# Four interleaved attention layers on one core: the builder orders VectorE's and GpSimd's latest instructions together in time

## The chip, the cores and the metric

One core of a Trainium2 chip. The metric is the device time of one execution in microseconds (us). Engines: TensorE (PE in the profile) multiplies and writes its results to banks of PSUM; its weight loads are PEld. ScalarE (ACT) evaluates exponentials, VectorE (DVE) and GpSimd (POOL) do elementwise work, SyncE (SP) issues transfers.

## The reference

An input x of 2048 tokens by 512 goes through four layers in turn, each x + f(layernorm(x)), with 32 heads of 16:

```python
x = x + _A_ref(_layernorm(x), A_wq, A_wk, A_wv, A_wo, A_beta)
x = x + _B_ref(_layernorm(x), B_wqkv, B_wo)
x = x + _A_ref(_layernorm(x), A_wq, A_wk, A_wv, A_wo, A_beta)
x = x + _B_ref(_layernorm(x), B_wqkv, B_wo)
```

B is plain attention over all 2048 tokens: softmax(q k^T / 4) v, then the output projection. A cuts the tokens into four segments of 512. Inside a segment it is causal attention; beside it stands a memory, read with phi(q) M / (phi(q) z) and then updated with phi(k)^T v, where phi(t) is t + 1 above zero and exp(t) below. A gate per head, sigmoid(beta), mixes the two. The segments of A are a chain through M and z; a segment of a layer needs only what the layer before it has finished.

## The kernel before, in words

Nothing of the program is written in its final order by hand. A Python class, `Builder`, walks through the work and calls `Sched.add` for each instruction; `Sched` keeps a list for each engine, finds what each instruction must wait for, and estimates on a model clock (`estimate`, line 128) when it would end. The builder's choices read this clock: `late("dve")`, for instance, is how far VectorE's model time is past TensorE's. The emitted program is the five lists; the clock itself leaves nothing in it.

**Units.** Scores are made in tiles of 128 keys by 512 queries for one head, one bank of PSUM each. A *unit* (`unit`, line 1752) is two or three tiles: their score products (`ps<-qm,KB` in layers 2 and 4, `ps<-qm,KA` in layers 1 and 3), then one exponential on ScalarE over all of them (line 1829, 1024 or 1536 wide) to the tile pT, then, two units later, the products with V. Two sets of three banks alternate, so a unit's scores wait for the exponential two units before.

**Tiles on VectorE.** When a unit has only two tiles for ScalarE, VectorE may take a tile or two into other banks (`dx_first`, line 1306). It reads the scores from PSUM, scales them and writes 16-bit integers whose bits are an approximation of the exponential (line 1314, 512 or 1024 wide). Two more versions of it are made by adding constants (`EXP_STEPS`), and TensorE multiplies all three with V and sums them: three products for such a tile, one for a tile of ScalarE. The buffers are dxt and, where they are free, borrowed ones named KA, QA, VA, wA and wB.

**The two additions** run on either engine. `task_dx` and `dx_four` (lines 1352, 1389) put them on VectorE (line 1370, 1024 integers for a pair of tiles; line 1403, 2048 for two pairs) unless `pool_copy` (line 1377) puts them on GpSimd (line 1385, 512 words of 32 bits, one instruction for each pair). It does so when GpSimd's model time is less than a limit, POOL_D or POOL_C, past VectorE's.

**Background work** comes between units: normalization, projections, the memory, output projections, loads. Tasks are generators that give up control with a price (`bg_one`, line 1482). Whether one may run next is decided by limits and by the model clock.

**Limits.** `PLAN` has one row for each 20 units (units 0 to 1528, rows 0 to 76). `set_limits` loads a row when its first unit begins: how late VectorE may be, how many tiles of a group it may take, when banks count as free, and some 60 more.

**The port.** VectorE and GpSimd can hold each other up. Before the change, `estimate` keeps the last eight intervals of GpSimd and the last sixteen of VectorE's instructions without PSUM (`held`, `taken`). An instruction that is added is moved behind an interval of the other engine that was added before it. It then stays where it is, even if an instruction that is added later to the other engine begins earlier in model time.

Of the kernel before, what the change touches and what calls it, by code (L numbers as in the profile page):

```python
# [7 lines left out]
ALU = mybir.AluOpType  # L8
# [3 lines left out]
D = 512  # L12
# [21 lines left out]
PORT = 140  # L34

LAG = {"pe": 100, "act": 60, "dve": 60, "pool": 70, "sp": 50}
# [51 lines left out]
class Sched:  # L88
# [4 lines left out]
    def __init__(self):  # L93
        self.ops = {e: [] for e in ENGS}
        self.t = {e: 0.0 for e in ENGS}
        self.tiles = []

        self.streams, self.cover = [], 0.0
        self.recent, self.over, self.pe_end, self.floor = [], [0.0, 0.0], 0.0, 0.0
        self.held, self.taken, self.port, self.raw = [], [], False, False  # L100
        self.pe_seen, self.pe_no, self.pe_at = {}, [0], [0.0]
# [261 lines left out]
class Builder:  # L363
# [15 lines left out]
        12: dict(R_LATE=1500, DX_LATE=500, REST=12, NEAR=8, R_NEAR=50, PV_SKIP=500, FILL_DVE=400, BUSY_ROOM=900, CR_W=1300, DX_LAG=1, LOW=20, HOLD_SEGS=2, BACK=6, R_PAIRS=2, TRADE=0, HOLD_MAX=0),
        13: dict(R_LATE=1500, DX_LATE=500, REST=12, NEAR=8, R_NEAR=50, PV_SKIP=500, FILL_DVE=400, BUSY_ROOM=900, CR_W=1300, DX_LAG=1, LOW=20, HOLD_SEGS=2, BACK=6, R_PAIRS=2, TRADE=0, HOLD_MAX=0),  # L380
        14: dict(MARGIN=500, NEAR=12, PV_SKIP=100, FILL_DVE=200, BUSY_ROOM=300, FILL=0.55, CR_W=1500, CARRY_W=400, R_PAIRS=2, OPART=3, GAP=3, DVE_LATE=800, QMIN=1, POOL_QM=1, SLACK=350, R_NEAR=10, CR_B=1800, QWAIT=8, LN1_AT=6, CR_A=1200, POOL_D=2500, POOL_WAIT=0),
        15: dict(MARGIN=500, NEAR=12, PV_SKIP=100, FILL_DVE=200, BUSY_ROOM=300, FILL=0.55, CR_W=1500, CARRY_W=400, R_PAIRS=2, OPART=3, GAP=3, DVE_LATE=800, QMIN=1, POOL_QM=1, PAIRS=999, SLACK=350, R_NEAR=10, CR_B=1800, QWAIT=8, LN1_AT=6, CR_A=1200, POOL_D=2500, POOL_WAIT=0, POOL_C=2000, PACE=12),
        16: dict(DX_BANK=900, SLACK=350, PV_SKIP=100, EARLY=100, FILL_DVE=200, BUSY_ROOM=300, BACK=6, FILL=0.55, CR_W=1500, PART=3, R_PAIRS=2, TAKEN=0.3, DVE_LATE=800, LN1_AT=6, BUSY_BACK=800, MARGIN=500, LOW=30, POOL_C=2000, OPART=3, GAP=3, PAIRS=24, R_NEAR=10, QWAIT=8, CR_A=1200, POOL_D=2500, PHI_LATE=0, QMIN=1, NEAR=12, POOL_QM=1),
        17: dict(MARGIN=400, NEAR=3, PV_SKIP=100, FILL_DVE=100, BUSY_ROOM=900, FILL=0.55, CR_W=1500, CARRY_W=400, R_PAIRS=2, OPART=4, GAP=3, DVE_LATE=800, QMIN=1, HOLD_AT=40, POOL_QM=1, ACT1=300, DX_LATE=900, REST=8, CR_B=1800, DX_LAG=1, BACK=6, QWAIT=3, POOL_C=2000, LOW=14, BUSY_WAIT=500, SLACK=350, PART=3, BUSY_BACK=800, R_NEAR=10, POOL_D=2500, PHI_LATE=0),
        18: dict(MARGIN=400, NEAR=3, PV_SKIP=100, FILL_DVE=100, BUSY_ROOM=900, FILL=0.4, CR_W=1500, CARRY_W=400, R_PAIRS=2, OPART=4, GAP=3, DVE_LATE=800, QMIN=1, HOLD_AT=40, POOL_QM=1, ACT1=300, DX_LATE=900, REST=8, CR_B=1800, DX_LAG=1, BACK=6, QWAIT=3, POOL_C=0, LOW=14, BUSY_WAIT=500, POOL_D=1200, PART=3, PHI_LATE=0, REST_A=20, EVAC_ACT=800),
        19: dict(MARGIN=400, NEAR=3, PV_SKIP=100, FILL_DVE=100, BUSY_ROOM=900, FILL=0.4, CR_W=1500, CARRY_W=400, R_PAIRS=2, OPART=4, GAP=3, DVE_LATE=800, QMIN=1, HOLD_AT=40, POOL_QM=1, ACT1=300, DX_LATE=900, REST=8, CR_B=1800, DX_LAG=1, BACK=6, QWAIT=3, POOL_C=0, LOW=14, BUSY_WAIT=500, POOL_D=1200, PART=3, PHI_LATE=0, REST_A=20, EVAC_ACT=800),
        20: dict(MARGIN=400, NEAR=3, PV_SKIP=100, FILL_DVE=100, BUSY_ROOM=900, FILL=0.4, CR_W=1500, CARRY_W=400, R_PAIRS=2, OPART=4, GAP=3, DVE_LATE=800, QMIN=1, HOLD_AT=40, POOL_QM=1, ACT1=300, DX_LATE=900, REST=8, CR_B=1800, DX_LAG=1, BACK=6, QWAIT=3, POOL_C=1, LOW=14, BUSY_WAIT=500, POOL_D=1200, PART=3, PHI_LATE=0, EVAC_ACT=800),
        21: dict(MARGIN=400, NEAR=3, PV_SKIP=100, FILL_DVE=100, BUSY_ROOM=900, FILL=0.4, CR_W=1500, CARRY_W=400, R_PAIRS=2, OPART=3, GAP=3, DVE_LATE=800, QMIN=1, HOLD_AT=40, POOL_QM=1, ACT1=300, DX_LATE=900, REST=8, CR_B=1800, DX_LAG=1, BACK=2, QWAIT=3, POOL_C=0, LOW=14, BUSY_WAIT=500, POOL_D=1200, R_NEAR=10),
        22: dict(DX_LATE=900, R_NEAR=10, EARLY=0, BUSY_ROOM=900, FILL=0.57, OPART=4, MASK_PE=200, DIV_LATE=2500, DVE_LATE=800, BG_BANK=400, QMIN=4, HOLD_SEGS=2, PHI_LATE=0, POOL_QM=1, DX_BANK=700, SLACK=700, BACK=6, PART=3, LN1_AT=3, BUSY_BACK=800, POOL_XN=1, NEAR=5, LOW=30, ACT1=300, REST=20, PV_SKIP=900, CR_B=1800, R_PAIRS=2, DX_LAG=1, QWAIT=3, CARRY_W=400, MARGIN=400, POOL_C=1),
# [62 lines left out]
    NEARW = 60  # L452
# [1793 lines left out]
```

## Time and profile before

| | |
|---|---|
| median of 3 runs | 1702.32 us (1701.98 to 1706.57) |
| profiled execution | 1705.54 us, span 1703.8 us |
| granted TensorE clock, mean | 0.997 |
| ScalarE busy | 1656.1 us, 97% of the span |
| TensorE busy | 1603.3 us, 94% |
| VectorE busy | 1472.4 us, 86% |
| GpSimd busy | 966.7 us, 57% |

A row of a group reads: line, engine, operation, output<-inputs, shapes, count | busy us, mean ns of one | idle time of the engine just before them, and what ended it. Neighbouring instructions of one engine overlap, so a mean can be longer than the distance from one start to the next. TensorE's busy time includes products with zeros that the builder puts into its gaps.

### The profile page before, as it was taken

The page shows a single profiled execution, that of the slowest core. Times are in us where ns is not written, and L with a number is a line of the kernel's source. Part 1 is how long each engine was busy: PE and PEld are TensorE (multiplying, and loading weights), DVE is VectorE, ACT ScalarE, POOL GpSimd, SP SyncE. Part 2 cuts the span into 40 slices and gives each one's busy share as a digit, 9 for nine tenths or more (in the row PEclk, how much of TensorE's full clock was granted, in tenths as well). Part 3 has the DMA queues.
Part 4 walks back from the last instruction along what each step waited for, and adds up shares of the span by engine and source line. Part 5 has one row for each costly group of instructions (what it writes and reads, how often), then busy time and mean ns, then how long its engine had stood idle before and what let it go on. Part 6 is the DMA issues. An engine that isn't in the chain of part 4 may idle for free.

```text
span 1703.8 us, 45449 instructions
## 1 busy us (share of the span) xinstructions
PE 1603.3 (94%) x19699; PEld 570.6 (33%) x19699; DVE 1472.4 (86%) x2555; ACT 1656.1 (97%) x1574; POOL 966.7 (57%) x1057
## 2 busy tenths in 40 slices
PE   8998989999999999999899999999999999999999
PEld 5553435322222232434235222432222222222226
DVE  6667776999999999887977899889999999999996
ACT  8899999999999999999899999999999999999998
POOL 2333212358966555411652865566688866668995
PEclk9999999999999999999999999999999999999999
DMA  6210201001112001222132112001001100100000
GB/s 180 39 21 20 46 13 36 5 14 23 23 21 52 17 14 33 55 68 51 48 60 30 31 38 53 14 14 51 2 17 20 45 17 17 14 10 17 17 14 18
DMA packets 148424, 54.46 MB, mean 32 GB/s; under 512 B 128768, under 2 KB 147712, under 8 KB 148224
## 3 DMA queue, kind: packets, MB, share of 16 engines
q1 hardware_dynamic: 148224, 51.56, 14.0%
q8 instruction: 154, 2.52, 0.6%
q14 instruction: 46, 0.38, 0.1%
HBM read 18.88 MB, written 2.10 MB: 12 GB/s over the span
## 4 chain that ended last, share of the span: by engine, by line
ACT 53%; PE 26%; DVE 16%; POOL 3%; issue 1%; DMA 0%; ACTq 0%; SPq 0%; POOLq 0%; DVEq 0%
ACT pT L1829 52%; PE ps L626 25%; DVE KA L1314 3%; DVE dxt L1314 3%; DVE wA L1314 1%; DVE wB L1314 1%; ACT amem L903 1%; DVE dxt L1370 1%; POOL dxt L1385 1%; DVE lnst L801 1%; POOL QA L1385 1%; DVE x L1152 0%; DVE xn L830 0%; DVE wB L1403 0%; POOL pT L1843 0%
## 5 line engine op out<-in xcount | busy, mean ns | idle before, releaser
L1829 ACT ACTIVATE pT<-ps 128x1024 bf16<-128x1024 f32 (+1 forms) x1529 | 1625.2, 1221 | 35.8 <-PE ps L626 31.4
L626 PE MATMUL ps<-qm,KB 32*128 32x512 bf16 x4096 | 566.3, 385 | 66.8 <-ACT pT L1829 42.0
L626 PE MATMUL ps<-pT,VB 128*17 128x512 bf16 x2810 | 485.7, 385 | 3.9 <-DVE ub L688 0.7
L1385 POOL TENSOR_TENSOR dxt<-dxt,shift 128x512 int32<-128x512 int32 (+1 forms) x237 | 252.3, 1074 | 244.1 <-DVE dxt L1370 128.7
L626 PEld LDWEIGHTS ps<-qm,KB 32*128 32x128 bf16 x4096 | 144.8, 91 | 584.3 <-ACT pT L1829 445.0
L1314 DVE TENSOR_SCALAR KA<-ps 128x512 uint16<-128x512 f32 (+1 forms) x424 | 310.9, 753 | 16.8 <-PE ps L626 15.1
L1314 DVE TENSOR_SCALAR dxt<-ps 128x512 uint16<-128x512 f32 (+1 forms) x341 | 249.8, 749 | 18.4 <-PE ps L626 17.0
L626 PE MATMUL ps<-dxt,VB 128*17 128x512 bf16 x1089 | 235.7, 382 | 0.2 <-POOL dxt L1385 0.2
L1385 POOL TENSOR_TENSOR VA<-KA,shift 128x512 int32<-128x512 int32 (+1 forms) x177 | 187.5, 1067 | 80.2 <-DVE QA L1370 43.1
L626 PEld LDWEIGHTS ps<-pT,VB 128*17 128x17 bf16 x2810 | 113.1, 87 | 280.2 <-issue 261.2
L1843 POOL TENSOR_SCALAR_AFFINE_SELECT pT<-pT 128x512 bf16<-128x512 bf16 (+4 forms) x134 | 73.9, 563 | 222.7 <-ACT pT L1829 222.7
L1385 POOL TENSOR_TENSOR QA<-KA,shift 128x512 int32<-128x512 int32 (+1 forms) x109 | 119.9, 1107 | 65.6 <-DVE KA L1314 62.4
L1385 POOL TENSOR_TENSOR wB<-wB,shift 128x512 int32<-128x512 int32 (+1 forms) x105 | 110.1, 1059 | 43.9 <-DVE wB L1370 17.8
L626 PE MATMUL ps<-QA,VB 128*17 128x512 bf16 x460 | 132.8, 383 | 0.0
L626 PE MATMUL ps<-VA,VB 128*17 128x512 bf16 x460 | 131.3, 382 | 0.5 <-POOL VA L1385 0.4
L1385 POOL TENSOR_TENSOR wA<-wA,shift 128x512 int32<-128x512 int32 (+1 forms) x94 | 101.8, 1092 | 42.9 <-DVE wA L1370 22.9
L1314 DVE TENSOR_SCALAR wB<-ps 128x512 uint16<-128x512 f32 (+1 forms) x157 | 115.4, 752 | 7.5 <-PE ps L626 7.1
L626 PE MATMUL ps<-KA,VB 128*17 128x512 bf16 x460 | 118.9, 383 | 0.0
L1314 DVE TENSOR_SCALAR wA<-ps 128x512 uint16<-128x512 f32 (+1 forms) x142 | 109.2, 786 | 7.2 <-PE ps L626 6.5
L626 PE MATMUL ps<-wA,VB 128*17 128x512 bf16 x486 | 113.0, 384 | 0.3 <-POOL wA L1385 0.2
L626 PE MATMUL ps<-wB,VB 128*17 128x512 bf16 x519 | 112.5, 390 | 0.1
L626 PE MATMUL ps<-qm,KA 32*128 32x128 bf16 (+2 forms) x1536 | 95.3, 254 | 13.7 <-ACT pT L1829 10.1
(172 smaller groups left out, 2166.6 us busy)
## 6 DMA issues: line engine op xcount, KB each, us to landing
wB<-in_B_wqkv_dram SPq DMA_DIRECT2D x48, 128.0 KB, 2.4
wA<-in_A_wk_dram SPq DMA_DIRECT2D x16, 128.0 KB, 2.3
wA<-in_A_wq_dram SPq DMA_DIRECT2D x16, 128.0 KB, 2.2
wA<-in_A_wv_dram SPq DMA_DIRECT2D x16, 128.0 KB, 2.4
out_dram<-x SPq DMA_DIRECT2D x8, 256.0 KB, 2.2
x<-in_A_x_dram SPq DMA_DIRECT2D x3, 512.0 KB, 9.4
wB<-in_B_wqkv_dram SPq DMA_DIRECT2D x1, 1536.0 KB, 12.8
oT<-ob SPq DMA_TRANSPOSE x63, 2.5
```

The lines of the kernel that those rows point to most:

```text
L626: self.sc.add("pe", lambda e: e.matmul(out, lhsT, rhs, start=start, stop=stop, skip_group_check=True), reads=reads, banks=[(bank, "w", all ...
L801: self.op("dve", (lambda i, t: lambda e: e.bn_stats(st[:, k, i, 0:6], self.x[:, t, :]))(i, t), reads=[self.b_x[t]], writes=[bs], ns=690, p ...
L903: self.op("act", lambda e: e.activation(et, src, ACT.Exp), reads=bsrc, writes=self.b_amem, ns=1023, gap=915)
L1314: self.op("dve", lambda e: e.tensor_scalar(d, o, SCALE * LOG2E * 128, 127.0 * 128 + EXP_BIAS, op0=ALU.mult, op1=ALU.add), writes=self.b_dx ...
L1370: self.op("dve", (lambda d, s, c: lambda e: e.tensor_scalar(d, s, float(c), None, op0=ALU.add))(d, s, c), reads=self.b_dxs[b][0:len(ents)] ...
L1385: self.op("pool", lambda e: e.tensor_tensor(d, s, c, ALU.add), reads=src + [self.b_shift] + [first] * k, writes=dst, ns=165 + 1.75 * n, ga ...
L1829: self.sc.add("act", (lambda dst, src: lambda e: e.activation(dst, src, ACT.Exp, scale=SCALE))(dst, src), writes=self.b_pT[slot * 3 + i:sl ...
L1843: self.op("pool", (lambda blk, pat: lambda e: e.affine_select(blk, blk, pattern=pat, compare_op=ALU.is_ge, fill=0.0, base=0, channel_multi ...
```

## The change

It alters the model clock, some modelled prices and the limits; no formula of the computation changes.

1. Each of VectorE and GpSimd keeps its latest six instructions in a queue. When an instruction that uses the port is added and the other engine's clock is past its start, `resolve` places both queues again, always the one that can start first. One that would start inside the other's interval is moved to 140 ns (VectorE) or 168 ns (GpSimd) before that interval's end.
2. Model prices: a GpSimd instruction's distance to the next is its length less 131 ns (85 before), for the additions 99 + 1.75 n (145 before), for the quotient `ob` 1080 (1250 before). ScalarE's start behind a TensorE product is modelled 60 ns earlier. One memset on GpSimd no longer counts as using the port.
3. `PLAN`: all but eight of the 77 rows are new.

```diff
-PORT = 140
+PORT, PORT_G, QUEUE = 140, 168, 6
...
-        ready = max([d.end + LAG[d.eng] if d.eng != e else d.end + 35 for d in op.deps] + [self.floor])
+        ready = max([d.end + LAG[d.eng] - 60 * (e == "act" and d.eng == "pe") if d.eng != e else d.end + 35 for d in op.deps] + [self.floor])
...
-            op.end = max(self.t[e] + gap, ready + ns)
-            if e == "pool":
-                for a, z in self.taken:
-                    if a < op.end - ns + 20 < z:
-                        op.end = z - 20 + ns
-                self.held = self.held[-7:] + [(op.end - ns, op.end)]
-            elif self.port:
-                for a, z in self.held:
-                    if a + 20 < op.end - ns < z - PORT:
-                        op.end = z - PORT + ns
-                self.taken = self.taken[-15:] + [(op.end - ns, op.end - 60)]
-            self.t[e] = op.end
+            if e == "act":
+                op.end = self.t[e] = max(self.t[e] + gap, ready + ns)
+                return
+            self.queue(e, [op, ns, gap, ready, self.lock, 0.0])
+
+    def queue(self, e, new):
+        o = "pool" if e == "dve" else "dve"
+        at = max(self.t[e] + new[2], new[3] + new[1])
+        mine, other = self.recent_ops[e], self.recent_ops[o]
+        mine.append(new)
+        if not new[4] or self.t[o] <= at - new[1]:
+            new[5] = new[0].end = self.t[e] = at
+        else:
+            self.resolve()
...
+    def resolve(self):
+        D, G = self.recent_ops["dve"], self.recent_ops["pool"]
...
+            if j == len(G) or i < len(D) and x <= y:
+                if r[4]:
+                    for a, z in lg:
+                        if a + 20 < x < z - PORT:
+                            x = z - PORT
+                    ld.append((x, x + r[1]))
...
+                if q[4]:
+                    for a, z in ld:
+                        if a < y < z - PORT_G:
+                            y = z - PORT_G
...
-        9: dict(R_LATE=1200, NEARW=40, PAIRS=24, MASK_PE=800, LEVEL=3, TAKEN=0.5, LOW=30, MARGIN=350, TAKEN_A=1, EARLY=300, OPART=3, FILL=0.47, DX_BANK=900, CR_A=1200, HOLD_SEGS=2),
+        9: dict(R_LATE=1200, NEARW=40, PAIRS=24, MASK_PE=800, LEVEL=3, TAKEN=0.5, LOW=30, MARGIN=350, TAKEN_A=1, EARLY=300, OPART=3, FILL=0.47, DX_BANK=900, CR_A=1200, HOLD_SEGS=2, HOLD_AT=40),
...
-        self.sc.port = bool(self.PORTS) and self.sc.raw
+        self.sc.lock = self.sc.raw if eng == "dve" else port
+        if eng == "pool" and gap is None:
+            gap = max(ns - 131, 60)
```

What the two programs hold, counted from their orders:

| | before | after |
|---|---|---|
| exponentials of scores, 1024 wide / 1536 wide | 1064 / 465 | 1082 / 448 |
| of these behind the last exponential of the memory features | 506 / 90 | 509 / 79 |
| exponentials ahead of the third layer's first one of the memory features | 572 | 442 |
| copies from PSUM on ScalarE (KA, VA, QA, KB, ub) | 3, 3, 2, 0, 0 | 2, 4, 3, 1, 2 |
| VectorE's tile reads, 512 / 1024 wide | 915 / 149 | 934 / 147 |
| additions on VectorE, 512 / 1024 / 2048 wide | 29 / 299 / 93 | 22 / 201 / 94 |
| additions on GpSimd, 512 / 256 words | 705 / 17 | 819 / 18 |
| of the 512-word ones behind the last fill of VB | 312 | 346 |
| products with V in layers 2 and 4 from pT / from the tile buffers (17x512) | 2810 / 3474 | 2793 / 3525 |

Line numbers after the change are 42 higher in this part of the program (1314 is 1356, 1370 is 1412, 1385 is 1427, 1403 is 1445, 1829 is 1871). Three places, before and then after.

ScalarE where the third layer's first exponential of the memory features stands (`amem<-phk`); the other rows are units:

```order
177 L1829 ACTIVATE pT<-ps 128x1024 x11
178 L1829 ACTIVATE pT<-ps 128x1536 x3
179 L1829 ACTIVATE pT<-ps 128x1024
180 L903 ACTIVATE amem<-phk 128x1024
181 L1829 ACTIVATE pT<-ps 128x1024 x3
182 L1829 ACTIVATE pT<-ps 128x1536 x2
183 L903 ACTIVATE amem<-phk 128x1024
```
```order
168 L1871 ACTIVATE pT<-ps 128x1536 x2
169 L1871 ACTIVATE pT<-ps 128x1024 x7
170 L945 ACTIVATE amem<-phk 128x1024
171 L1871 ACTIVATE pT<-ps 128x1024 x2
172 L1871 ACTIVATE pT<-ps 128x1536
173 L1871 ACTIVATE pT<-ps 128x1024
174 L945 ACTIVATE amem<-phk 128x1024
```

The neighbourhood reads alike; what moved is its place, from behind 572 exponentials of units to behind 442.

VectorE late in the fourth layer, some 190 rows before its end before the change and 90 after it:

```order
2010 L1314 TENSOR_SCALAR KA<-ps 128x512
2011 L1370 TENSOR_SCALAR VA<-KA 128x1024
2012 L1314 TENSOR_SCALAR KA<-ps 128x512 x2
2013 L1370 TENSOR_SCALAR wB<-wB 128x1024
2014 L1314 TENSOR_SCALAR KA<-ps 128x512
2015 L1370 TENSOR_SCALAR QA<-KA 128x1024
```
```order
2018 L1356 TENSOR_SCALAR KA<-ps 128x512
2019 L1445 TENSOR_SCALAR VA<-KA 128x2048
2020 L1356 TENSOR_SCALAR KA<-ps 128x512 x2
2021 L1356 TENSOR_SCALAR dxt<-ps 128x512
2022 L1356 TENSOR_SCALAR dxt<-ps 128x1024
2023 L1356 TENSOR_SCALAR dxt<-ps 128x512
```

Three single additions among four tile reads before; one double addition and then five reads in a row after.

GpSimd at its end, the last additions (`shift` holds the constants):

```order
668 L1385 TENSOR_TENSOR VA<-KA,shift 128x512 x4
669 L1385 TENSOR_TENSOR dxt<-dxt,shift 128x512 x2
670 L1385 TENSOR_TENSOR QA<-KA,shift 128x512
671 L1385 TENSOR_TENSOR VA<-KA,shift 128x512
672 L1385 TENSOR_TENSOR QA<-KA,shift 128x512
```
```order
706 L1427 TENSOR_TENSOR VA<-KA,shift 128x512
707 L1427 TENSOR_TENSOR QA<-KA,shift 128x512
708 L1427 TENSOR_TENSOR VA<-KA,shift 128x512
709 L1427 TENSOR_TENSOR QA<-KA,shift 128x512 x2
710 L1427 TENSOR_TENSOR dxt<-dxt,shift 128x512 x3
711 L1427 TENSOR_TENSOR QA<-KA,shift 128x512 x2
```

QA and VA are a pair's two additions. More of them stand on GpSimd together now, where before one of the two was often VectorE's.

More of the change, by code (lines that the diff above doesn't have):

```diff
@@ L99, in __init__ @@
         self.recent, self.over, self.pe_end, self.floor = [], [0.0, 0.0], 0.0, 0.0
-        self.held, self.taken, self.port, self.raw = [], [], False, False
+        self.recent_ops, self.locks, self.base = {"dve": [], "pool": []}, {"dve": [], "pool": []}, {"dve": 0.0, "pool": 0.0}
+        self.lock, self.raw = False, False
         self.pe_seen, self.pe_no, self.pe_at = {}, [0], [0.0]
@@ L164, in estimate @@
-            self.t[e] = op.end
+            if e == "act":
[11 more added lines that the diff above has]
+            self.resolve()
+        if len(mine) > QUEUE:
+            r = mine.pop(0)
+            self.base[e] = r[5]
+            if r[4]:
+                self.locks[e] = self.locks[e][-3:] + [(r[5] - r[1], r[5])]
@@ new lines, in resolve @@
+    def resolve(self):
+        D, G = self.recent_ops["dve"], self.recent_ops["pool"]
+        i = j = 0
+        pd, pg = self.base["dve"], self.base["pool"]
+        ld, lg = list(self.locks["dve"]), list(self.locks["pool"])
+        while i < len(D) or j < len(G):
+            if i < len(D):
+                r = D[i]
+                x = max(pd + r[2], r[3] + r[1]) - r[1]
+            if j < len(G):
+                q = G[j]
+                y = max(pg + q[2], q[3] + q[1]) - q[1]
+            if j == len(G) or i < len(D) and x <= y:
+                if r[4]:
+                    for a, z in lg:
+                        if a + 20 < x < z - PORT:
+                            x = z - PORT
+                    ld.append((x, x + r[1]))
+                pd = r[5] = r[0].end = x + r[1]
+                i += 1
+            else:
+                if q[4]:
+                    for a, z in ld:
+                        if a < y < z - PORT_G:
+                            y = z - PORT_G
+                    lg.append((y, y + q[1]))
+                pg = q[5] = q[0].end = y + q[1]
+                j += 1
+        self.t["dve"], self.t["pool"] = pd, pg
@@ new lines @@
+        11: dict(R_LATE=1500, DX_LATE=900, REST=12, NEAR=8, TAKEN_A=1, R_NEAR=50, PV_SKIP=500, FILL_DVE=400, BUSY_ROOM=900, CR_W=1300, DX_LAG=1, LOW=20, HOLD_SEGS=2, BACK=6, R_PAIRS=2, PACE=12, BG_BANK=100),
+        12: dict(R_LATE=1500, DX_LATE=900, REST=12, NEAR=8, R_NEAR=50, PV_SKIP=500, FILL_DVE=400, BUSY_ROOM=900, CR_W=1300, DX_LAG=1, LOW=20, HOLD_SEGS=2, BACK=6, R_PAIRS=2, TRADE=0, HOLD_MAX=0, BUSY_BACK=800, ACT1=200),
+        13: dict(MARGIN=500, NEAR=12, PV_SKIP=100, FILL_DVE=200, BUSY_ROOM=300, FILL=0.55, CR_W=1500, CARRY_W=400, R_PAIRS=2, OPART=3, GAP=3, DVE_LATE=800, QMIN=1, POOL_QM=1, SLACK=350, R_NEAR=10, CR_B=1800, QWAIT=8, LN1_AT=6, CR_A=1200, POOL_D=2500, POOL_WAIT=0, RUSH0=40),
@@ L1063, in v @@
                     yield list(need), 0, 0
-                self.op("pool", (lambda on: lambda e: e.memset(on, 1.0))(on), writes=[bv])
+                self.op("pool", (lambda on: lambda e: e.memset(on, 1.0))(on), writes=[bv], port=False)
                 yield from self.proj_tm(self.wB, self.b_wB[2], 1024, slot, ti, self.v_evac(vt, bv))
@@ L1384, in pool_copy @@
         c = bcast(self.shift[:, k:k + 1], [[0, n]])
-        self.op("pool", lambda e: e.tensor_tensor(d, s, c, ALU.add), reads=src + [self.b_shift] + [first] * k, writes=dst, ns=165 + 1.75 * n, gap=145 + 1.75 * n)
+        self.op("pool", lambda e: e.tensor_tensor(d, s, c, ALU.add), reads=src + [self.b_shift] + [first] * k, writes=dst, ns=165 + 1.75 * n, gap=99 + 1.75 * n)
         self.cr_dve += 350
```

135 lines of the change are left out of this document (66 added, 69 removed).

## The prediction

> **What bounds the kernel now.** I read the page's busy table and its chain first, then ScalarE's groups with the shapes kept apart, then stretches of 200 us, then the waits of VectorE and GpSimd.
>
> ```profile
> span 1703.8 us, 45449 instructions
> PE 1603.3 (94%) x19699; PEld 570.6 (33%) x19699; DVE 1472.4 (86%) x2555; ACT 1656.1 (97%) x1574; POOL 966.7 (57%) x1057
> ACT 53%; PE 26%; DVE 16%; POOL 3%; issue 1%; DMA 0%; ACTq 0%; SPq 0%; POOLq 0%; DVEq 0%
> L1829 ACT ACTIVATE pT<-ps 128x1024 bf16<-128x1024 f32 (+1 forms) x1529 | 1625.2, 1221 | 35.8 <-PE ps L626 31.4
> ```
>
> ScalarE is busy for all but 47.7 of 1703.8 us, nearly all of it with the 1529 exponentials of line 1829. The chain goes through ScalarE for only half of the span: scores, exponential and release of the banks hand over to each other, and a quarter of the chain is TensorE's. So ScalarE's work is the floor, and lateness of TensorE, or of VectorE through the banks it reads, is added on top.
>
> The next view keeps ScalarE's shapes apart; behind it stand two unbroken runs of exponentials from the timeline (start, length, count), one all 1024 wide and one all 1536 wide.
>
> ```profile
> L1829 ACT ACTIVATE pT<-ps 128x1024 bf16<-128x1024 f32 x1064 | 1016.4, 1098 | 16.9 <-PE ps L626 14.6
> L1829 ACT ACTIVATE pT<-ps 128x1536 bf16<-128x1536 f32 x465 | 660.6, 1503 | 18.8 <-PE ps L626 16.9
> L686 ACT ACTIVATE KA<-ps 128x512 bf16<-128x512 f32 x3 | 1.8, 600 | 2.3 <-PE ps L626 2.3
> ```
> ```profile
> 995.78 14.77 ACT L1829 ACTIVATE pT<-ps 128x1024 bf16<-128x1024 f32 x16
> 169.24 14.88 ACT L1829 ACTIVATE pT<-ps 128x1536 bf16<-128x1536 f32 x11
> ```
>
> Neighbours overlap, so the means (1098, 1503 ns) are not what one costs. In an undisturbed run one costs 14.77 / 16 = 0.923 us, a wide one 14.88 / 11 = 1.353 us. All of them need 1064 x 0.923 + 465 x 1.353 = 1611 us; the group was busy 1625.2 and idle 35.8. So some 14 us of late starts hide inside "busy", beside the idle time.
>
> Where is the idle time? Stretches of 200 us, columns PE, PEld, DVE, ACT, POOL, and then one wait in the stretch from 798 to 862 us:
>
> ```profile
> 0.00:200.00 200.00, 182.68 (x2628) 92.89 (x2628) 135.04 (x319) 185.47 (x154) 62.90 (x110) 1.00 0.27 62
> 200.00:400.00 200.00, 185.82 (x2450) 69.39 (x2451) 163.09 (x311) 197.25 (x173) 68.28 (x87) 1.00 0.09 18
> 400.00:600.00 200.00, 190.08 (x1900) 50.42 (x1892) 190.29 (x297) 196.99 (x201) 144.01 (x142) 0.99 0.14 30
> 600.00:800.00 200.00, 189.98 (x2623) 79.68 (x2620) 167.38 (x334) 198.51 (x183) 77.26 (x104) 1.00 0.19 41
> 800.00:1000.00 200.00, 187.92 (x2403) 69.49 (x2404) 171.64 (x303) 193.05 (x181) 117.69 (x119) 1.00 0.22 46
> 1000.00:1200.00 200.00, 189.03 (x2292) 64.94 (x2291) 175.33 (x320) 196.88 (x186) 112.36 (x123) 1.00 0.14 32
> 1200.00:1400.00 200.00, 189.13 (x1961) 50.36 (x1961) 188.39 (x286) 194.47 (x201) 155.98 (x161) 0.98 0.10 20
> 1400.00:1600.00 200.00, 191.73 (x1957) 50.40 (x1950) 195.45 (x272) 197.68 (x205) 148.49 (x144) 1.00 0.08 16
> 1600.00:1800.00 200.00, 96.98 (x1513) 43.05 (x1509) 85.77 (x123) 95.78 (x100) 79.71 (x74) 0.99 0.03 8
> ```
> ```profile
> ACT pT L1829 <- PE ps L626: 5.3, 9, 1.4
> ```
>
> ScalarE idles 14.5 us in the first stretch and 8.0 in the last (103.8 - 95.8): start and end, which I hold fixed. The rest is 2.8 + 3.0 + 1.5 + 7.0 + 3.1 + 5.5 + 2.3 = 25.2 us, and most of the 7.0 are nine waits for TensorE where the third layer begins. Two faces show: from 400 to 600 and from 1200 to 1600 VectorE is full (94 to 98%); from 600 to 800 GpSimd works only 77 of 200 us and VectorE 167.
>
> **The change, part by part.** The new clock of the builder emits nothing itself; it and the new limits choose another order. I counted the two orders.
>
> *ScalarE.* Its exponentials go from 1064 of 1024 and 465 of 1536 to 1082 and 448; 15 score tiles go to VectorE. That is 18 x 0.923 - 17 x 1.353 = -6.4 us. It gains four copies out of the banks (VA, QA, KB one each, ub two, KA one fewer) at 0.600: +2.4. ScalarE's work: -4.0 us, all on the path. After the last exponential of the memory features it is 596 -> 588 instructions of line 1829, 90 -> 79 of them wide: the late stretch gets 11 x 1.353 - 3 x 0.923 = 12.1 us lighter there, the part before it heavier.
>
> *VectorE and GpSimd.* The two cheap integer additions that follow each tile sit on either engine. Their rows:
>
> ```profile
> L1370 DVE TENSOR_SCALAR dxt<-dxt 128x1024 uint16<-128x1024 uint16 x105 | 63.5, 613 | 1.4
> L1370 DVE TENSOR_SCALAR QA<-KA 128x1024 uint16<-128x1024 uint16 x83 | 44.4, 537 | 1.3
> L1370 DVE TENSOR_SCALAR wA<-wA 128x1024 uint16<-128x1024 uint16 x46 | 27.2, 597 | 0.7
> L1370 DVE TENSOR_SCALAR wB<-wB 128x1024 uint16<-128x1024 uint16 x33 | 19.1, 583 | 0.3
> L1370 DVE TENSOR_SCALAR VA<-KA 128x1024 uint16<-128x1024 uint16 x32 | 20.0, 626 | 0.5
> L1314 DVE TENSOR_SCALAR KA<-ps 128x512 uint16<-128x512 f32 x367 | 244.0, 681 | 12.3 <-PE ps L626 11.1
> L1314 DVE TENSOR_SCALAR KA<-ps 128x1024 uint16<-128x1024 f32 x57 | 69.5, 1219 | 4.5 <-PE ps L626 4.0
> L1385 POOL TENSOR_TENSOR dxt<-dxt,shift 128x512 int32<-128x512 int32 x229 | 247.3, 1088 | 237.4 <-DVE dxt L1370 122.0 <-DVE dxt L1314 95.7 <-DVE dxt L1403 16.6
> ```
> ```profile
> L1370 DVE TENSOR_SCALAR wB<-wB x37: 408/434/1275, 394.1 to 1566.1; 128x1024 uint16<-128x1024 uint16 x33, 128x512 uint16<-128x512 uint16 x4
> L1385 POOL TENSOR_TENSOR VA<-KA,shift x177: 607/1037/1488, 305.9 to 1690.3; 128x512 int32<-128x512 int32 x175, 128x256 int32<-128x256 int32 x2
> ```
>
> The 299 VectorE additions average 174.2 / 299 = 583 ns against a median of 434: some are stretched, up to 1275 ns, by a GpSimd instruction under way. The new order has 201, so 98 x 0.583 = 57 us leave VectorE; 19 more tile reads of 512 and 2 fewer of 1024 bring 19 x 0.681 - 2 x 1.219 = 10.5 back, and the four copies are 2.7 less. VectorE falls by about 49 us, to some 1423. GpSimd gets 114 more additions at 1.088: +124 us, to some 1091, 64% of the span.
>
> By the Trainium skill (SBUF — State Buffer, "SBUF: two separate sides") the shared pair of ports is an exclusive lock that one side holds for its whole instruction while the other fully blocks. By that rule an addition of 434 ns could last 434 + 1037 = 1471 ns here, but the longest seen is 1275, so the wait ends before the other's instruction does. By the rule, a third of the 201 additions left, 67, would wait 0.2 us longer, 13 of the 49 us that VectorE gains; the relief below would be worth 6 us instead of 8, and the sum -8 instead of -10.
>
> In the late dense stretch, as the change's section shows, three additions between the tile reads become one double addition: the reads that free the score banks stand closer together.
>
> *What relief is worth.* VectorE is off ScalarE's path except through the banks, so its 49 us are not a gain; their worth lies between nothing and the 25.2 idle plus 14 hidden us (below nothing only by new waits, which is a rival below). The full stretches 400 to 600 and 1200 to 1600 hold 10.8 of the 25.2; the third layer's start holds most of another 7.0, and there the order changes too: its first exponential of the memory features comes after 442 exponentials instead of 572, so its projections lie beside more tile work. Its transposes on the SP queue and their VectorE reads move along; what covers them is the attention that is still left. I take a third of 25.2, nearest to the 7.0 row: -8 us.
>
> *TensorE.* A tile that VectorE takes is multiplied with V three times instead of once; the orders show 34 more such products in the second and fourth layers (17 fewer from pT, 51 more from the tile buffers).
>
> ```profile
> 605.08 0.60 PE L626 MATMUL ps<-wB,VB 128*17 128x512 bf16 x5
> 605.97 0.38 PE L626 MATMUL ps<-wB,VB 128*17 128x512 bf16 x1
> ```
>
> Five take 0.60 us and one 0.38, so a further set of up to four adds 0.22: 34 x 0.055 = 1.9 us well packed, 34 x 0.22 = 7.5 us alone. They stand in packs, so I take +2.
>
> Sum: -6.4 + 2.4 - 8 + 2 = -10 us. The profiled execution took 1705.5 us, 1.7 more than its span and 3.2 above the median of 1702.3; subtracting from that median gives 1692 us.
>
> **The rivals.**
>
> *Nothing measurable.* The relief goes to time that was covered: the chain puts VectorE at 16% and GpSimd at 3%, and only 31.4 us of ScalarE's waits have TensorE as releaser. Then -4.0 + 2 = -2 us, 1700. A form of it is that the new clock doesn't say when the two engines really hold the port.
>
> *A larger gain.* The third layer's start and the full stretches lose most of their waits: 20 of the 39 us, with -2: 1680. For it speaks the low GpSimd share from 600 to 800; against it that every order of this kernel has such seams.
>
> *Slower: GpSimd's additions come late.* One addition lasts 1037 on GpSimd and 434 ns on VectorE, a tile pair needs two, and a group can close only with all its products. So far TensorE hardly ever waits for an addition (the last column):
>
> ```profile
> L626 PE MATMUL ps<-dxt,VB 128*17 128x512 bf16 x1089 | 235.7, 382 | 0.2 <-POOL dxt L1385 0.2
> ```
>
> The Trainium skill (GPSIMD Engine Reference, "Key points") says that for elementwise work VectorE is about twice as fast, which speaks against the change; this trace has 2.4. If one in six of the 114 moved additions arrives late by the 0.6 us of difference, that is 19 x 0.6 = 11 us; with -2 from the rest, 1711. It decides where GpSimd has no idle time to catch up: in the last 504 us it was busy 156.0 + 148.5 + 79.7 = 384 us, 76%. Behind its last fill of VB it gets 34 more additions, 37 us, which makes 84%, so some room is left.
>
> *Seams moved, not removed.* ScalarE's part before the last memory features is heavier by 12.1 - 6.4 = 5.7 us and two copies, and it could meet a busier TensorE there; this only narrows the gain and lies in the range.
>
> **How the numbers follow.** Forecast (1692, own range 1685 to 1697): 0.50. Larger gain (1680): 0.14. Nothing measurable (1700): 0.21. Slower (1711): 0.15. A measurement of this kernel tells about 0.3% from no change, 5.1 us: faster is below 1697.2, slower above 1707.4. The forecast and the larger gain lie below, and a little of the forecast's upper edge falls inside: faster 0.63, same 0.22, slower 0.15. The range takes the forecast, nothing measurable, the near half of the larger gain and the near part of slower: 1679 to 1707.
>
> **What would show it.** Right: ScalarE's group at 1082 and 448 and about 6 us less undisturbed work, VectorE near 1423 us, GpSimd near 1090, the idle time before the exponentials down from 35.8 to about 28, and no group of nine waits at the third layer's start. Wrong: new waits of TensorE's products for GpSimd (nearly none now), a wait of ScalarE in the dense stretches that grew, or the same idle time under a smaller ScalarE sum, which is the rival of nothing measurable.

## The result, and the profile after

The changed kernel takes 1687.3 us (median of 4 runs, 1685.0 to 1688.4) where the kernel before took 1703.8 on the same chip: a ratio of 0.990 (95% interval 0.988 to 0.992), 16.5 us. The forecast was 10 us, in a range from 23 less to 5 more. The page of the profiled execution:

```profile
span 1686.6 us, 45464 instructions
PE 1591.7 (94%) x19648; PEld 570.0 (34%) x19715; DVE 1440.7 (85%) x2462; ACT 1648.3 (98%) x1579; POOL 1093.4 (65%) x1186
ACT 61%; PE 27%; DVE 10%; DMA 1%; issue 1%; POOL 0%; SPq 0%; ACTq 0%; POOLq 0%
L1871 ACT ACTIVATE pT<-ps 128x1024 bf16<-128x1024 f32 (+1 forms) x1530 | 1615.8, 1223 | 24.8 <-PE ps L666 22.0
```

The group of exponentials, in two shapes, and VectorE's additions:

```profile
L1871 ACT ACTIVATE pT<-ps 128x1024 bf16<-128x1024 f32 x1082 | 1031.9, 1105 | 10.1 <-PE ps L666 8.7
L1871 ACT ACTIVATE pT<-ps 128x1536 bf16<-128x1536 f32 x448 | 636.6, 1506 | 14.7 <-PE ps L666 13.3
```
```profile
L1412 DVE TENSOR_SCALAR dxt<-dxt 128x1024 uint16<-128x1024 uint16 x67 | 44.3, 662 | 1.3
L1412 DVE TENSOR_SCALAR QA<-KA 128x1024 uint16<-128x1024 uint16 x48 | 29.9, 626 | 0.9
L1412 DVE TENSOR_SCALAR VA<-KA 128x1024 uint16<-128x1024 uint16 x32 | 19.5, 610 | 0.5
L1412 DVE TENSOR_SCALAR wA<-wA 128x1024 uint16<-128x1024 uint16 x33 | 19.5, 592 | 0.6
L1412 DVE TENSOR_SCALAR wB<-wB 128x1024 uint16<-128x1024 uint16 x21 | 14.6, 704 | 0.3
```

ScalarE is idle for 1686.6 - 1648.3 = 38.3 us, 47.7 before: 9.4 less. At the prediction's prices its exponentials need 1082 x 0.923 + 448 x 1.353 = 1604.8 us undisturbed, 6.4 less; they were busy 1615.8, so by this estimate 11.0 us of late starts are hidden in there, 14.0 before. With the four copies (+2.4) that is -6.4 + 2.4 - 9.4 - 3.0 = -16.4 of the span's -17.2.

Where did it go? Both programs have a mark that is the same work: ScalarE's last exponential of the memory features. The rows give its kind with the first and last start:

```profile
L903 ACT ACTIVATE amem<-QA x12: 1048/1117/1187, 96.4 to 1093.5; 128x1024 bf16<-128x1024 bf16 x12
```
```profile
L945 ACT ACTIVATE amem<-QA x12: 1057/1095/1228, 95.5 to 1090.7; 128x1024 bf16<-128x1024 bf16 x12
```

Only 2.8 us are gained ahead of the mark, 14.4 behind it. The stretches ahead and behind, with columns as before (PE, PEld, DVE, ACT, POOL), first of the kernel before, then of the changed one:

```profile
0.00:1093.50 1093.50, 1024.70 (x12993) 390.43 (x12993) 910.63 (x1717) 1062.34 (x974) 521.29 (x614) 1.00 0.18 39
1093.50:1703.80 610.30, 578.64 (x6710) 180.18 (x6709) 561.75 (x838) 593.75 (x601) 445.41 (x444) 0.99 0.09 20
```
```profile
0.00:1090.70 1090.70, 1026.30 (x13087) 395.44 (x13149) 889.70 (x1676) 1067.48 (x985) 607.23 (x714) 1.00 0.19 39
1090.70:1686.60 595.90, 565.35 (x6565) 174.58 (x6566) 551.03 (x787) 580.87 (x595) 486.21 (x473) 0.99 0.09 20
```

Behind the mark ScalarE has 12.9 us less to do (593.75 to 580.87) and idles 1.5 less (16.6 to 15.0). Ahead of it, it has 5.1 more to do and idles 7.9 less (31.2 to 23.2). These are two different gains. The second one has its largest piece between the second and the third segment of the third layer, 789 to 887 us before and 660 to 894 after. ScalarE's waits there:

```profile
ACT pT L1829 <- PE ps L626: 5.9, 11, 1.4
```
```profile
ACT pT L1871 <- PE ps L666: 0.6, 3, 0.2
```

In the kernel before, that stretch holds 82 exponentials of units beside its background work, in the changed one 231. The same projections and normalizations lie beside more than twice the attention, and TensorE is late by 0.6 us instead of 5.9. That the one causes the other is read off the two traces; no run tested it by itself.

### The profile page after: what moved, and what is told of

It is laid out like the page before. It is cut to its first block, busy times and chain, and to the rows that moved or that the text cites. A ratio compares the mean times of both kernels' runs of the same rounds, so it can differ in the third digit from the quotient of the medians.

```text
span 1686.6 us, 45464 instructions
## 1 busy us (share of the span) xinstructions
PE 1591.7 (94%) x19648; PEld 570.0 (34%) x19715; DVE 1440.7 (85%) x2462; ACT 1648.3 (98%) x1579; POOL 1093.4 (65%) x1186
## 4 chain that ended last, share of the span: by engine, by line
ACT 61%; PE 27%; DVE 10%; DMA 1%; issue 1%; POOL 0%; SPq 0%; ACTq 0%; POOLq 0%
ACT pT L1871 60%; PE ps L666 27%; DVE KA L1356 2%; DVE dxt L1356 1%; DVE wA L1356 1%; ACT amem L945 1%; DMA tb<-ub 1%; DVE lnst L843 0%; DVE wB L1356 0%; DVE wA L1412 0%; DVE x L1194 0%; DMA xT<-xn 0%; DVE VA L1412 0%; DVE dxt L1412 0%; DVE QA L1412 0%
## 5 line engine op out<-in xcount | busy, mean ns | idle before, releaser
L1871 ACT ACTIVATE pT<-ps 128x1024 bf16<-128x1024 f32 (+1 forms) x1530 | 1615.8, 1223 | 24.8 <-PE ps L666 22.0
L1356 DVE TENSOR_SCALAR KA<-ps 128x512 uint16<-128x512 f32 (+1 forms) x426 | 316.5, 764 | 22.5 <-PE ps L666 20.0
L1356 DVE TENSOR_SCALAR dxt<-ps 128x512 uint16<-128x512 f32 (+1 forms) x316 | 229.0, 743 | 20.6 <-PE ps L666 19.1
L1427 POOL TENSOR_TENSOR QA<-KA,shift 128x512 int32<-128x512 int32 x163 | 181.0, 1119 | 68.2 <-DVE KA L1356 68.2
L666 PE MATMUL ps<-dxt,VB 128*17 128x512 bf16 x999 | 213.8, 384 | 0.5 <-POOL dxt L1427 0.5
L1885 POOL TENSOR_SCALAR_AFFINE_SELECT pT<-pT 128x256 bf16<-128x256 bf16 (+4 forms) x146 | 75.7, 533 | 195.9 <-ACT pT L1871 195.7
L1427 POOL TENSOR_TENSOR wA<-wA,shift 128x512 int32<-128x512 int32 (+1 forms) x148 | 160.4, 1095 | 62.7 <-DVE wA L1412 31.1
L1356 DVE TENSOR_SCALAR wA<-ps 128x512 uint16<-128x512 f32 (+1 forms) x206 | 146.0, 726 | 13.7 <-PE ps L666 12.9
L1427 POOL TENSOR_TENSOR wB<-wB,shift 128x512 int32<-128x512 int32 (+1 forms) x116 | 124.8, 1087 | 34.4 <-DVE wB L1356 28.6
L666 PE MATMUL ps<-wA,VB 128*17 128x512 bf16 x651 | 140.4, 384 | 0.0
L1356 DVE TENSOR_SCALAR wB<-ps 128x512 uint16<-128x512 f32 (+1 forms) x133 | 104.5, 798 | 8.5 <-PE ps L666 7.6
L666 PE MATMUL ps<-VA,pT 128*128 128x34 bf16 (+1 forms) x2520 | 105.0, 188 | 2.7 <-DVE ob L1968 1.6
```

Source lines behind the costliest of these rows:

```text
L666: self.sc.add("pe", lambda e: e.matmul(out, lhsT, rhs, start=start, stop=stop, skip_group_check=True), reads=reads, banks=[(bank, "w", all ...
L1356: self.op("dve", lambda e: e.tensor_scalar(d, o, SCALE * LOG2E * 128, 127.0 * 128 + EXP_BIAS, op0=ALU.mult, op1=ALU.add), writes=self.b_dx ...
L1427: self.op("pool", lambda e: e.tensor_tensor(d, s, c, ALU.add), reads=src + [self.b_shift] + [first] * k, writes=dst, ns=165 + 1.75 * n, ga ...
L1871: self.sc.add("act", (lambda dst, src: lambda e: e.activation(dst, src, ACT.Exp, scale=SCALE))(dst, src), writes=self.b_pT[slot * 3 + i:sl ...
L1885: self.op("pool", (lambda blk, pat: lambda e: e.affine_select(blk, blk, pattern=pat, compare_op=ALU.is_ge, fill=0.0, base=0, channel_multi ...
```

## The experiments

The theory of the prediction was that VectorE's relief (additions moved to GpSimd) is worth a share of ScalarE's stalls, whatever else the order does. Its rivals: relief is covered; GpSimd's additions come late; what counts is one exact order, to which the limits are fitted. A first group of kernels keeps every list of instructions in its order and only changes the engine of some additions: each is put into the other engine's list at the place where the builder created it, and all waits are derived anew. A second group changes the clock or the limits and so the whole order. The ratio is always to the kernel before, timed on the same chip; the changed kernel's is 0.990, and a difference of 0.001 is 1.7 us.

### 114 additions back to VectorE, in the changed order

```diff
+    MOVE, PAIR, COUNT = ("pool", "dve"), 2, 114
...
+        self.move()
         self.sc.finalize()
```

> The changed kernel, every list in the same order, but 114 of GpSimd's 512-word additions (57 pairs of tiles, spread evenly) are done by VectorE at the place where they were created. Exponentials, tiles and background work stay where they are. VectorE gets 114 x 0.64 = 73 us of additions, more than the change took away, GpSimd loses about 124. If VectorE's relief carries the gain, the time goes back by 8 us or more, to 1695 or above, and ScalarE's idle time grows from 38 us to over 46, most of it where VectorE is full (1200 to 1600 us). If the relief is covered, the time stays within 5 us of 1687.

1733.9 us, ratio 1.016 (1.014 to 1.019): 45 us are lost, more than five times the 8 us that the prediction gave to relief. (Its runs had a lower granted TensorE clock, 0.985 to 0.995; but a run of each kernel at 0.995 took 1730.2 and 1688.2 us, 42 apart.) The page, ScalarE's group, and TensorE's waits for VectorE's tile reads, with those of the changed kernel behind them:

```profile
PE 1627.2 (94%) x19715; PEld 576.2 (33%) x19715; DVE 1497.6 (86%) x2576; ACT 1657.9 (95%) x1579; POOL 980.3 (56%) x1072
L1878 ACT ACTIVATE pT<-ps 128x1024 bf16<-128x1024 f32 (+1 forms) x1530 | 1624.8, 1195 | 66.7 <-PE ps L670 61.8
PEld ps L670 <- DVE KA L1360: 34.6, 65, 1.5
PEld ps L670 <- DVE dxt L1360: 24.1, 45, 2.0
PEld ps L670 <- DVE wA L1360: 17.5, 33, 1.9
```
```profile
PEld ps L666 <- DVE KA L1356: 19.8, 47, 1.2
PEld ps L666 <- DVE dxt L1356: 12.8, 32, 1.6
PEld ps L666 <- DVE wA L1356: 8.6, 22, 0.8
```

The line of waiting shows whole: an addition on VectorE stands ahead of a tile read, the read frees its bank later, TensorE waits for the bank (76.2 us on these three rows instead of 41.2), and ScalarE waits for TensorE (61.8 instead of 22.0). The trace tells which reads they are: 39 of the 57 pairs have a tile read directly behind them in VectorE's list. TensorE waits 36.7 us for reads that stand at most three places behind a moved addition, and 47.4 us for all the others, where the changed kernel has 45.5 for all reads. VectorE is only 86% busy in it. One part of the expectation missed: ScalarE's idle time grew from 38.3 to 80.2 us, but not mostly from 1200 to 1600 us, where 18 of the 42 us lie; another 17 lie from 600 to 1200. So the relief isn't covered; but this tells what it costs to take relief out of an order that counts on it, and not yet what giving it is worth.

### 98 additions to GpSimd, in the order before

```diff
+    MOVE, PAIR, COUNT = ("dve", "pool"), 1, 98
```

> The kernel before, every list in the same order, but 98 of VectorE's 299 additions of 1024 are done by GpSimd. VectorE loses about 57 us, GpSimd gets about 106. If relief alone is worth what I gave it, the time falls from 1703 to about 1695. If it is covered, 1703 within 5. If GpSimd's longer additions come too late in an order that wasn't made for them, TensorE waits for GpSimd (now 0.2 us for the largest group) and the time rises to 1710 or more.

The 98 are additions whose pair already had its other addition on GpSimd.

1719.6 us, ratio 1.007 (1.005 to 1.009): slower by 12 us, though VectorE falls from 1472 to 1445 us. The page, ScalarE's group and the row of the largest group of products with V, and TensorE's longest waits for GpSimd's additions:

```profile
PE 1609.5 (94%) x19699; PEld 571.9 (33%) x19699; DVE 1445.0 (84%) x2457; ACT 1659.3 (97%) x1574; POOL 1062.4 (62%) x1155
L1835 ACT ACTIVATE pT<-ps 128x1024 bf16<-128x1024 f32 (+1 forms) x1529 | 1627.9, 1209 | 47.2 <-PE ps L630 41.8
L630 PE MATMUL ps<-dxt,VB 128*17 128x512 bf16 x1089 | 239.4, 384 | 3.8 <-POOL dxt L1391 3.7
PEld ps L630 <- POOL dxt L1391: 9.1, 14, 1.1
PEld ps L630 <- POOL VA L1391: 5.8, 10, 1.1
PEld ps L630 <- POOL wB L1391: 5.7, 8, 1.4
PEld ps L630 <- POOL wA L1391: 4.7, 7, 1.5
```

This is the rival of late additions: products that were ready when TensorE reached them now hold it up (0.2 us before on the same group's row, 3.8 now), and ScalarE idles 47.2 us ahead of its exponentials instead of 35.8. But mostly it is not the moved additions that come late. All waits of TensorE's weight loads for GpSimd's additions, first in the kernel before, then here for the additions that were GpSimd's already (line 1391), then for the 98 moved (line 1377), in us and times:

```profile
  PEld ps L626: 7.0, 17
  PEld ps L630: 27.6, 43
  PEld ps L630: 3.5, 11
```

That points to GpSimd's queue: a moved addition delays what stands behind it, as one on VectorE delays the tile reads behind it. Of the 27.6 us, 17.2 are at additions at most five places behind a moved one, where 46% of them stand. Seen by time, 19.5 of the 27.6 lie from 400 to 500, 1200 to 1400 and 1600 to 1700 us, where GpSimd is 87 to 94% busy. The theory in its simple form falls here: relief alone, in the order of before, has a negative price.

### Fewer moved, in both directions

The changed order again, `COUNT` 28 back to VectorE, and in another kernel 40 more to GpSimd.

> The changed kernel in its order, with 28 additions (14 pairs, spread evenly) given back to VectorE, a quarter of the 114 that cost 1733.9 - 1687.3 = 46.6 us. If each addition on VectorE pushes back the tile reads behind it, the cost is in proportion: 28 / 114 x 46.6 = 11 us, 1699. If VectorE has room for some and the cost starts beyond it, 1687 to 1691.

1697.3 us, ratio 0.9954 (0.9937 to 0.9971): 0.54% or 9 us above the changed kernel, a quarter of the additions for a fifth of the cost. It is in proportion.

> The changed kernel in its order, with 40 more of VectorE's additions given to GpSimd, 161 left of 201. VectorE loses about 25 us, GpSimd gets 43. If more relief of VectorE is more gain, 1680 to 1684. If the order is balanced and a late addition now holds TensorE up, as in the kernel before with 98 moved (12.9 us, 0.13 each), 40 x 0.13 = 5 us: 1692.

1700.8 us, ratio 0.9974 (0.9963 to 0.9985): 0.74% or 13 us above the changed kernel, more than the 5 expected. ScalarE's group, the row of the products, and the new waits:

```profile
L1877 ACT ACTIVATE pT<-ps 128x1024 bf16<-128x1024 f32 (+1 forms) x1530 | 1619.4, 1211 | 34.9 <-PE ps L670 29.8
L670 PE MATMUL ps<-dxt,VB 128*17 128x512 bf16 x999 | 214.9, 384 | 6.6 <-POOL dxt L1419 5.5
PEld ps L670 <- POOL dxt L1419: 7.6, 5, 2.3
```

Here the moved additions themselves (line 1419) hold the weight loads up for 10.3 us, and GpSimd's others for 14.7 (5.2 in the changed kernel), 8.2 of them at most five places behind a moved one, where 20% of these additions stand. An addition moved either way loses 0.3 us. For such moves the changed order stands at a minimum between two waits: tile reads that come late behind VectorE's additions, and products that come late behind GpSimd's.

### The same 28 additions, early or late

```diff
-            new.tag = id(src[0].last_write), lambda e: e.tensor_scalar(u, v, cc, None, op0=ALU.add)
+            new.tag = (id(src[0].last_write), lambda e: e.tensor_scalar(u, v, cc, None, op0=ALU.add)) if self.LATE == (self.step > 942) else None
```

> The changed kernel in its order, 28 additions (14 pairs) given back to VectorE, all ahead of unit 943, where VectorE is busy 81.6% (889.7 of 1090.7 us). If an addition costs by how full VectorE is, little there: 1687 to 1692. If every placement is fitted to the order alike, as much as spread evenly (10 us): 1697.

1698.5 us, ratio 0.9966 (0.9953 to 0.9978): 11 us above the changed kernel.

> The same with 28 additions behind unit 942, where VectorE is busy 92.5% (551.0 of 595.9 us). If an addition costs by how full VectorE is, more than spread evenly: 28 x 0.64 = 18 us on an engine with little room, 1700 to 1705. If every placement is fitted alike, 1697.

1702.5 us, ratio 0.9989 (0.9979 to 0.9999): 15 us above it. ScalarE's group in both, early first:

```profile
L1878 ACT ACTIVATE pT<-ps 128x1024 bf16<-128x1024 f32 (+1 forms) x1530 | 1618.3, 1210 | 32.0 <-PE ps L670 28.1
```
```profile
L1878 ACT ACTIVATE pT<-ps 128x1024 bf16<-128x1024 f32 (+1 forms) x1530 | 1617.2, 1214 | 37.1 <-PE ps L670 34.1
```

Late took 4 us longer than early, and the two intervals just don't touch. That this is the fuller engine is not shown, because the TensorE clock that the chip granted differs too: 0.996 to 0.999 in the five runs of early, 0.990 to 0.996 in the eleven of late. Within the late kernel the time goes with it, 1699.4 us at 0.996 and 1707.1 at 0.990; at 0.996, three runs of early took 1698.3 to 1700.6. In the trace the loss is a few spells at half clock, of which this is one of the two longest in late (the clock, 0.50, is the third number from the end):

```profile
1356.45:1363.20 6.75, 6.50 (x43) 1.24 (x41) 4.47 (x7) 3.74 (x4) 2.75 (x3) 0.50 0.10 19
```

Up to its last 10 us late has four such spells, and early three. In them and in the 4 us behind each, ScalarE waits 11.5 and 5.6 us for TensorE; outside them 22.6 and 22.5. The three rows of waits for tile reads come to 50.4 us in late and 50.2 in early (41.2 in the changed kernel). Why late gets the lower clock stays open. What stands is that early costs 0.4 us an addition with VectorE at 82%, against an expectation of nearly nothing. That points to the place in the queue, which matters on an engine with idle time too.

### The clock alone, the limits alone, and one number of the clock

The new clock with `PLAN` of before; the old clock with the new `PLAN`; and the changed kernel with

```diff
-PORT, PORT_G, QUEUE = 140, 168, 6
+PORT, PORT_G, QUEUE = 150, 168, 6
```

> The new clock and prices with the old limits. The order has 1009 exponentials of 1024 and 521 of 1536, 25 tiles and more for ScalarE than before: 1009 x 0.923 + 521 x 1.353 = 1636 us undisturbed, 25 more than the 1611 of before. If the clock alone brought the gain, 1703 or less. If clock and limits only fit together, 1728 or more, since stalls are not tuned away either.

1739.7 us, ratio 1.019 (1.017 to 1.022).

> The old clock and prices with the new limits: 1034 exponentials of 1024 and 488 of 1536, 1615 us undisturbed, 4 more than before. If the limits carry the gain whatever the clock, 1703 or less. If they fit the new clock only, ScalarE's stalls grow with the work: 1715 to 1745.

1759.8 us, ratio 1.031 (1.028 to 1.034), beyond what was expected.

> The new clock and the new limits, with one number of the clock another: an instruction of VectorE may start 150 ns before the end of GpSimd's interval, 140 in the change. What the chip does is not different. The order has 1047 exponentials of 1024 and 478 of 1536, 1613 us undisturbed, 8 more than the changed kernel. If the gain comes from a clock that knows the lock, 10 ns matter little: 1687 to 1697. If the limits are fitted to one exact order, it is lost: 1715 or more.

1728.3 us, ratio 1.013 (1.011 to 1.016). The group of exponentials of these three, in the same order:

```profile
L1871 ACT ACTIVATE pT<-ps 128x1024 bf16<-128x1024 f32 (+1 forms) x1531 | 1648.0, 1248 | 47.7 <-PE ps L666 43.7
```
```profile
L1829 ACT ACTIVATE pT<-ps 128x1024 bf16<-128x1024 f32 (+1 forms) x1522 | 1641.2, 1196 | 70.6 <-PE ps L626 63.4
```
```profile
L1871 ACT ACTIVATE pT<-ps 128x1024 bf16<-128x1024 f32 (+1 forms) x1525 | 1631.0, 1218 | 47.5 <-PE ps L666 41.3
```

Ten nanoseconds in the builder's assumption, with nothing else different, cost 2.3%, more than twice the whole gain. Nor is 150 a worse figure than 140, by the last section's trace. The third run is the control for the other two: in all three, limits under another clock than their own give an order that nothing was fitted to, with 20 to 73 more tiles on ScalarE than the changed kernel's 3508 and two to three times its idle time. That the clock alone and the limits alone are slower therefore says nothing against either. It also means that these runs can't tell how much of the 16.5 us a truer picture of the port gave, and how much came from choosing the limits again.

### The late limits of before

Rows 57 to 76 of `PLAN` as before, all else as changed; up to unit 1140 the order is the changed one.

> The new clock, with the limits of before from row 57 on (units 1140 to the end, the last 390). Everything ahead of that, the third layer's start too, is the changed kernel's order. It has 1081 exponentials of 1024 and 454 of 1536: 998 + 614 = 1612 us undisturbed, 7 more. If the late, dense stretch carries most of the gain, 1697 or more. If the gain lies ahead of it, 1687 to 1692.

1695.4 us, ratio 0.9942 (0.9923 to 0.996), 0.42% or 7 us above the changed kernel, with its group of exponentials:

```profile
L1871 ACT ACTIVATE pT<-ps 128x1024 bf16<-128x1024 f32 (+1 forms) x1535 | 1623.3, 1221 | 24.9 <-PE ps L666 21.3
```

The idle time is the changed kernel's (24.9, 24.8); what came back is 7.5 us of ScalarE's work. By this run the new limits of the last 390 units bring exponentials that VectorE takes, and GpSimd does 28 additions fewer without them. That is less than half of the 16.5 us; the rest was won ahead of unit 1140. The control above bears on this too: rows 57 to 76 of before were not fitted to an order that begins like this, so 7 us may overstate what the new ones bring.

## Why the prediction was right, and where it wasn't

**ScalarE's work, -4.0.** Right: the counts are those of the orders, and at the prediction's prices they make -6.4 and +2.4. That the late part gets 12.1 us lighter shows as 12.9 behind the mark, that the part ahead gets heavier as 5.1.

**VectorE and GpSimd.** GpSimd came out at 1093 (1091 forecast), VectorE at 1441 instead of 1423. The additions left on VectorE average 127.8 / 201 = 0.636 us where the step took 0.583, 11 of the missing 18 us; the double ones, 2048 wide, rose from 79 to 85 us. With GpSimd at 65% of the span an addition is held up longer on average. The waiting of the 1024-wide ones as a whole hardly moved, (0.583 - 0.434) x 299 = 45 us before, (0.636 - 0.434) x 201 = 41 after, and GpSimd's 512-word additions still average 1094 ns (1088 before) against a median of 1037. A clock that knows the lock did not make the two engines collide less.

**The relief, -8.** The term that was mis-sized: idle and hidden late starts fell by 9.4 + 3.0 = 12.4 us. Its reason was also too simple. It priced relief as a thing of its own, between nothing and the stalls; with the order held still, relief made the kernel before slower by 12 us. The price belongs to order and placement together. The third of 25.2 us was a choice and not a derivation, so that the time came out inside the range is in part luck.

**The seam.** The nine waits between 798 and 862 us do go, as the step said, but they were put down to the start of the third layer. Its first exponential of the memory features starts at 676.9 us; the waits lie behind the second segment's last one (788.8 us). The count 572 to 442 tells of it only indirectly: the third segment stays nearly where it was (behind 745 exponentials of units, now 762), so the earlier start of the first two makes the room. The count that bears on the waits is 82 to 231 exponentials between the second and the third segment.

**TensorE, +2.** Not to be seen by itself: its busy time fell with the span, and ScalarE waits less for it. What 34 more products cost lies inside the smaller waits.

**The rivals.** *Nothing measurable* is out: the waits on TensorE fell from 31.4 to 22.0. *Slower by late additions* didn't happen, the row of the largest group waits 0.5 us for GpSimd (0.2 before), but the mechanism is real: the waits for GpSimd's additions grow where the kernel before gets slower with 98 moved and the changed one with 40. It priced the moved addition's own 0.6 us, while with 98 moved it is mostly GpSimd's other additions that come late. Its point of decision, that GpSimd has no idle time to catch up, holds for most of that run's waits, but not only in the last 504 us (7.5 of 27.6 us lie from 400 to 500); and it isn't enough by itself, since the changed kernel's GpSimd is 93% busy from 700 to 800 and from 1200 to 1300 us and TensorE waits less than 1 us for it there. *A larger gain* had nearly the right places and too large a size.

**Open.** How much a clock with the lock in it is worth by itself. A new choice of limits under the old clock would tell it; that wasn't made. Nor does a run tell what a neutral change of place would cost in the fixed order, one that moves nothing to another engine. And why some orders get a lower granted clock is not known.

## What to carry to other kernels

When a scheduler's limits are searched for, the result is one exact order; test a part by changing that order in one place with everything else held still, and run a meaningless change of the model as a control before blaming a part that was tried alone. Work that moves to a slower engine relieves the first one and delays whoever reads its result or one queued behind it, so its price has two signs, and here the busy share of neither engine over the span told which wins. Ask for each moved instruction what stands directly behind it in its queue. And compare the granted clock before explaining a few us.

## What the runs showed of the hardware

A VectorE addition of 1024 integers, 434 ns undisturbed, was stretched up to 1293 ns by GpSimd's additions of 1037 ns:

```profile
L1412 DVE TENSOR_SCALAR dxt<-dxt x79: 258/492/1293, 29.7 to 1669.0; 128x1024 uint16<-128x1024 uint16 x67, 128x512 uint16<-128x512 uint16 x12
```

The longest before the change was 1293 ns too (the prediction's 1275 is of another row), so again none lasted the 1471 ns that waiting for a whole instruction would make. One from the trace, start and length in us, and GpSimd's addition beside it:

```profile
808.19 1.29 DVE L1412 TENSOR_SCALAR dxt<-dxt 128x1024 uint16<-128x1024 uint16 x1
808.16 1.04 POOL L1427 TENSOR_TENSOR wB<-wB,shift 128x512 int32<-128x512 int32 x1
```

VectorE's ends 0.28 us behind GpSimd's. All 40 additions of this kind that lasted over 900 ns in the changed kernel end 282 to 287 ns behind the GpSimd instruction beside them, wherever in it they began, and all 37 in the kernel before 282 to 289. Undisturbed they need 420 to 434 ns, so by this estimate they go on some 135 to 150 ns before the end that the trace gives for GpSimd's: 140 and 150 in the builder's clock both fit.

And with no engine above 98% busy, single additions of 0.64 us given back to VectorE lengthened the span by 0.3 to 0.4 us each (9 us for 28, 11 for 28 ahead of unit 943, 45 for 114): half or more of a small delay on VectorE came through, though it has only 10% of the chain.
